# A gated MLP's first product with seven multiplications per block pair: running sums kept in PSUM, copied out between terms

## Chip, cores and metric

The kernel runs on one core of one Trainium2 chip. The metric is the device time of one execution in microseconds; lower is better. Three executions of the kernel before were timed.

## What is computed

The reference runs three layers one after the other on 8 sequences of 576 tokens: a memory attention over 8 heads of 64, a channel mix with token shift, and a gated MLP. The change touches the first product of the last one, `x @ w_in`, cut here to what matters:

```python
h = np.maximum(x @ w_in, 0.0)              # 576 x 512 times 512 x 1024, for each of 8 sequences
u, v = h[..., :512], h[..., 512:]
v_n = (v - mean(v)) / np.sqrt(var(v) + 1e-06)      # over the 512 columns
v_s = einsum('ts,bsd->btd', w_spatial, v_n) + b_spatial[None, :, None]
out = (u * v_s) @ w_out
```

## The kernel before

All matrix products are made in single precision from pairs of rounded values: each operand is split into a high and a low part, and a product is the sum of high times high, low times high and high times low (`three`, line 104). TensorE adds the terms up in a PSUM bank (`gemm`, line 95); `start=True` on the first matmul makes it overwrite the bank. A split (line 116) is a copy on ScalarE and a subtraction on VectorE.

The first 600 us hold the attention and the channel mix. The gated MLP follows, a sequence at a time: `uv(n)` makes the v half and then the u half of `x @ w_in`, `spatial` (line 975) the product over tokens, `project` (line 1003) the last product. Of each sequence 512 tokens go through `uv(b)`; the 64 left over from all eight are collected in one more call, `uv(B)`, called "rest", which runs behind sequence 0's. So there are nine calls, eighteen halves.

A half is two groups (`Group`, line 837), each a 256 x 512 by 512 x 512 product done with Winograd's form of Strassen's method: seven products of half-size blocks (128 x 256 by 256 x 256, numbered 1 to 7) in place of eight, and sums of them. A group's four results are c11 = 1 + 2, c12 = 1 + 6 + 5 + 3, c21 = 1 + 6 + 7 + 4 and c22 = 1 + 6 + 7 + 5, with numbers standing for products. `products` (line 940) runs over the seven in the order 1, 6, 2, 7, 5, 3, 4 and at each of these seven places over the two groups, so a half has fourteen steps. A step (line 844) is six matmuls of 128 x 128 by 128 x 256 into a bank of its own, taken from the eight in turn (`mm`), and then the sums in SBUF: product 1 is copied by ScalarE (line 854), product 5 too (line 862); products 6, 2, 7, 3 and 4 are added by VectorE (line 851) to what stands in SBUF; and product 5's copy is added to c12 and to c22 by GpSimd, or by VectorE in the u half of sequence 0 (`engine`, line 961).

When a v group is through, `done` (line 928) normalises its two row tiles (`layer_norm`, line 824: Relu, statistics, square root, and scaling on ScalarE and VectorE in turn, with one buffer for each small result) and splits them. These run while TensorE makes the u half. In the u half the result is only needed by the product over tokens.

After the third and the sixth place a chunk of the previous sequence's `project` (twelve matmuls of 288 columns) is put between as a filler. In the halves of sequence 0 and of "rest" there is none; there `turn` issues splits of the token weights and of the next operands. `load_x2` (line 601) fetches and splits the seven left or right operands; GpSimd makes the differences. `issue_after(copied[0].ins)` keeps some of the splits behind the last copy out of PSUM on ScalarE's queue. Apart from that the framework orders the instructions of each engine ahead of time, by their place in the program and by when it reckons them ready; each engine then runs its list strictly in that order, waiting on semaphores.

Of the kernel before, what the change touches and what calls it, by code (L numbers as in the profile page):

```python
# [12 lines left out]
ACTF = mybir.ActivationFunctionType  # L13
ALU = mybir.AluOpType
# [13 lines left out]
HALF = 256  # L28
# [15 lines left out]
def kernel(  # L44
# [18 lines left out]
    nc = tc.nc  # L63
# [9 lines left out]
    def bank(n):  # L73
        return ps.tile([128, 512], F32, tag=f"bank{n}", name=f"bank{n}")
# [17 lines left out]

        return tile_of(f"xs{n}", [128, 2 * HB if n == 7 else 4 * HALF], F32R)

    def gemm(out, pairs, part=0, parts=1):

        n = len(pairs)
        for i in range(part * n // parts, (part + 1) * n // parts):
            x = nc.tensor.matmul(  # L99
                out=out, lhsT=pairs[i][0], rhs=pairs[i][1], start=i == 0, stop=i == n - 1  # L100
            )
        return x

    def three(ah, al, bh, bl):

        return [*zip(ah, bh), *zip(al, bh), *zip(ah, bl)]
# [302 lines left out]
    mm = turns(0, 1, 2, 3)  # L409
# [62 lines left out]
    for c in ORDER:  # L472
        if c == "W":
            fetch_w_k()
        elif c == "w":
            part, ms = next(w_k_parts)
# [7 lines left out]
        elif c == "M":  # L484
# [3 lines left out]
                out=mu_sb[:, 2 * KC:], in0=mu_sb[:, 0:2 * KC], scalar1=-1.0, scalar2=1.0,  # L488
                op0=ALU.mult, op1=ALU.add,
            )  # L490
        else:
            n, late = "CKQDLR".index(c.upper()), c.islower()
# [32 lines left out]
    def w_in_steps():  # L525


        chunks = w_in.bitcast(U32).rearrange("(c p) f -> p c f", p=128)

        def parts_of(tag, parts):  # L530
            tiles = pair(tag, [128, 4096])
            wi_tiles.extend(tiles)
            parts.extend(t[:, 0:3584].rearrange("p (q c f) -> p q c f", q=7, c=2) for t in tiles)

        def add(out, a, b, op=ALU.subtract):
            nc.gpsimd.tensor_tensor(out=out, in0=a, in1=b, op=op)

        def part(p, half, j):
            f0 = p * DM + half * HALF + j * 128
            return chunks[:, :, 2 * f0:2 * f0 + 256]  # L540

        quads = tile_of("xT0", [128, 2, KC, HALF])
        for half in range(2):
            for j in range(2):
                load_f64(part(0, half, j), raw=quads[:, half, :, 128 * j:128 * j + 128])
                yield
                yield
        while not att_free:
            yield
        room = tile_of("asp", [128, 1792])  # L550
        parts_of("AT", wi_v)
        for j in range(2):
            at = []
            for half in range(2):
                at.append(load_f64(part(1, half, j)))
                yield
            (a11, a12), (a21, a22) = ((v[:, 0:2], v[:, 2:4]) for v in at)
            h, lo = (p[:, :, :, 128 * j:128 * j + 128] for p in wi_v)
            raw = room[:, 0:768].rearrange("p (q c f) -> p q c f", q=3, c=2)
            add(raw[:, 0], a21, a22, ALU.add)  # L560
            add(raw[:, 1], raw[:, 0], a11)
            add(raw[:, 2], a11, a21)
            for q, a in ((0, a11), (1, a12), (2, a22), (3, raw[:, 0]), (4, raw[:, 1]), (5, raw[:, 2])):
                split(a, h[:, q], lo[:, q])
                if q % 2:
                    yield
            add(raw[:, 0], a12, raw[:, 1])
            split(raw[:, 0], h[:, 6], lo[:, 6])
            yield
        a11, a12, a21, a22 = (quads[:, half, 2 * k:2 * k + 2] for half in range(2) for k in range(2))  # L570
        s1, s2, s4 = (room[:, 512 * n:512 * n + 512].rearrange("p (c f) -> p c f", c=2) for n in range(3))
        add(s1, a21, a22, ALU.add)
        add(a21, a11, a21)
        yield
        add(s2, s1, a11)
        add(s4, a12, s2)
        yield
        while not xT_free:
            yield
        chunks = w_out.bitcast(U32).rearrange("(c p) f -> p c f", p=128)  # L580
        wo_raw = tile_of("xT1", [128, KC, DM])
        for f0 in range(0, DM, 128):
            load_f64(chunks[:, :, 2 * f0:2 * f0 + 256], raw=wo_raw[:, :, f0:f0 + 128])
            yield
        while not w2_free:
            yield
        wo.extend(pair("W2", [128, KC, DM]))
        for c in range(KC):
            split(wo_raw[:, c], wo[0][:, c], wo[1][:, c])
            yield  # L590
        parts_of("W1", wi_u)
        for q, a in ((0, a11), (4, s2), (1, a12), (5, a21), (3, s1), (6, s4), (2, a22)):
            split(a, wi_u[0][:, q], wi_u[1][:, q])
            yield

# [5 lines left out]
    def load_x2(n):  # L601
# [33 lines left out]
        def put(q, x):  # L635
            ts[q] = place(q)

            with tc.issue_after(copied[0].ins) if rest or (n == 0 and xs_free) else nullcontext():
                split(x, *ts[q])

        if rest:
            for x in ((b11, 0, 0), (b21, 1, 0), (b12, 0, 1), (b22, 1, 1)):
                fetch_x2(*x)
            yield
            tiles = [tile_of(tag, [128, FC * HB], F32R) for tag in ("kh", "kl")]
            slots.update(zip((0, 1, 2, 4), [t[:, 4 * HALF * k:4 * HALF * (k + 1)] for t in tiles for k in range(2)]))
            put(0, b11)
            minus(b11, b12, b11)
            minus(b12, b22, b12)
            yield  # L650
            put(2, b22)
            minus(b22, b22, b11)
            yield
            put(4, b22)
            yield
            put(1, b21)
            minus(b21, b21, b22)
            yield
            while not late_free:
                yield  # L660
            yield
            put(5, b12)
            yield
            put(3, b11)
            yield
        else:
            for x in ((b12, 0, 1), (b11, 0, 0), (b21, 1, 0), (b22, 1, 1)):
                fetch_x2(*x)
            yield
            put(0, b11)  # L670
            minus(b11, b12, b11)
            yield
            put(1, b21)
            minus(b12, b22, b12)
            yield
            put(2, b22)
            minus(b22, b22, b11)
            yield
            put(4, b22)
            minus(b21, b21, b22)  # L680
            while not xs_free:
                yield
            while left_v:

                yield
            yield
            put(5, b12)
            yield
            put(3, b11)
            yield  # L690
        put(6, b21)
        x2s[n] = [ts[q] for q in range(7)]
# [94 lines left out]
    mm = turns(*range(8))  # L787
# [49 lines left out]
    class Group:  # L837

        def __init__(self, at, out, done, engine=nc.gpsimd):
            self.at, self.out, self.done, self.engine = at, out, done, engine

        def step(self, q):
            c11, c12, c21, c22 = self.out
            acc = bank(next(mm))[:, 0:HALF]
            a, b = self.at(q)
            gemm(acc, three(*a, *b))

            def add(engine, dst, x, y):  # L850
                engine.tensor_tensor(out=dst, in0=x, in1=y, op=ALU.add)  # L851

            if q == 1:
                copied[0] = nc.scalar.activation(out=c11, in_=acc, func=ACTF.Copy)
            elif q == 6:
                add(nc.vector, c12, acc, c11)
            elif q == 2:
                add(nc.vector, c11, acc, c11)
            elif q == 7:
                add(nc.vector, c21, acc, c12)  # L860
            elif q == 5:
                copied[0] = nc.scalar.activation(out=c22, in_=acc, func=ACTF.Copy)
                add(self.engine, c12, c22, c12)
                add(self.engine, c22, c22, c21)
            elif q == 3:
                add(nc.vector, c12, acc, c12)
            else:
                add(nc.vector, c21, acc, c21)
                self.done()


# [3 lines left out]
    def uv(n, fillers):  # L875
# [62 lines left out]
            return done  # L938

        def products(groups, after=lambda at_: None):  # L940
            for at_, q in enumerate((1, 6, 2, 7, 5, 3, 4)):
                for g in groups:
                    g.step(q)
                    turn()
                after(at_)
                if at_ in (2, 5):
                    f = next(fillers, None)
                    if f is not None:
                        f()
# [7 lines left out]
        def u_half(after=lambda at_: None):  # L957
            u = u_rest if rest else u_main
            products([
                Group(u_at(m), [u[:, f + m, s:s + HALF] for f in (0, 2) for s in (0, HALF)], lambda: None,  # L960
                      nc.vector if n == 0 else nc.gpsimd)
                for m in range(2)
            ], after)

# [183 lines left out]
```

## Time and profile before

| | |
|---|---|
| median of three runs | 1012.88 us (1010.77 to 1013.5) |
| span of the profiled execution | 1013.0 us |
| instructions | 20477 |
| TensorE matmuls, weight loads | 989.3 us (98%), 964.3 us (95%) |
| VectorE | 681.0 us (67%) |
| ScalarE | 608.5 us (60%) |
| GpSimd | 113.5 us (11%) |
| DMA | 87.83 MB, mean 87 GB/s |

The span runs from the first to the last instruction. PE stands for TensorE's matmuls, PEld for its weight loads, DVE for VectorE, ACT for ScalarE, POOL for GpSimd. Matmuls overlap: one of 256 columns has a row of 0.28 us, but the next starts some 0.11 us after it. A row of the timeline can merge several instructions of one form; "x4" says how many. What stands in brackets behind a row is the idle time before it and what ended it.

### The profile page before, as it was taken

Reading aid. Unit: us, or ns where it says so; the run is one execution under the profiler, and the core shown is the slowest. Engines: PE = TensorE matmul, PEld = TensorE weight load, DVE = VectorE, ACT = ScalarE, POOL = GpSimd, SP = SyncE. Lnnn points to the kernel's source line nnn. Section 1 sums busy time; section 2 is a strip of 40 time slices with the busy share of each in tenths; the row PEclk is TensorE's granted clock in tenths of the full one; section 3 lists DMA queues with packets and bytes.
Section 4 is the critical chain, followed back from the end, with each engine's and each line's share of the span. In section 5 each row is a group of like instructions: output and inputs, shape, how many; then the busy total and the mean of one; then the engine's idle time right before and its main releaser. Section 6 shows DMA issues by size and latency. Waiting matters only on the chain.

```text
span 1013.0 us, 20477 instructions
## 1 busy us (share of the span) xinstructions
PE 989.3 (98%) x8192; PEld 964.3 (95%) x8192; DVE 681.0 (67%) x1525; ACT 608.5 (60%) x1277; POOL 113.5 (11%) x124
## 2 busy tenths in 40 slices
PE   5889999999999999999999999999999999999998
PEld 4778999999999999999999999999999999999998
DVE  4999965675576567556667577986575757575763
ACT  4797885676678668657756475655354444445352
POOL 0000000000000000000022021412231313122220
PEclk9999999999999999999999999999999999999999
DMA  9686532233223322330042311202111111121101
GB/s 267 164 276 237 148 100 71 80 114 109 65 85 106 121 78 64 114 109 24 6 149 66 107 45 36 89 30 60 36 56 36 54 36 60 37 65 57 40 25 47
DMA packets 65135, 87.83 MB, mean 87 GB/s; under 512 B 8848, under 2 KB 57360, under 8 KB 62992
## 3 DMA queue, kind: packets, MB, share of 16 engines
q1 hardware_dynamic: 65040, 86.53, 27.6%
q8 instruction: 64, 1.05, 0.4%
q14 instruction: 31, 0.25, 0.1%
HBM read 67.77 MB, written 18.74 MB: 85 GB/s over the span
## 4 chain that ended last, share of the span: by engine, by line
PE 80%; ACT 8%; DVE 7%; DMA 3%; issue 1%; SPq 0%; POOL 0%; ACTq 0%; POOLq 0%; DVEq 0%
PE bank L99 77%; PE bank L271 2%; DMA st<-in_w_in 1%; DMA ATh<-in_kv 1%; DVE xs L118 1%; ACT t L712 1%; ACT kh L117 1%; ACT xs L117 1%; ACT t L710 1%; PE bank L323 1%; ACT xT L382 1%; DMA st<-x2d 0%; DVE kl L118 0%; ACT st L145 0%; ACT x32a L416 0%
## 5 line engine op out<-in xcount | busy, mean ns | idle before, releaser
L99 PE MATMUL bank<-xs,W1h 128*128 128x288 f32 (+1 forms) x1496 | 244.5, 292 | 1.8 <-DVE o L749 1.2
L99 PEld LDWEIGHTS bank<-xs,W1h 128*128 128x128 f32 x1496 | 210.4, 188 | 6.9 <-issue 5.8
L99 PE MATMUL bank<-xs,W1l 128*128 128x288 f32 (+1 forms) x748 | 135.5, 290 | 0.0
L99 PEld LDWEIGHTS bank<-xs,W1l 128*128 128x128 f32 x748 | 110.7, 188 | 0.2 <-issue 0.2
L118 DVE TENSOR_TENSOR kl<-t,kh 128x576 fp32r<-128x576 f32 x64 | 49.3, 771 | 58.5 <-ACT kh L117 57.9
L99 PE MATMUL bank<-xs,W2h 128*128 128x288 f32 x512 | 83.9, 298 | 1.3 <-ACT t L710 0.6
L710 ACT ACTIVATE t<-bank 128x288 f32<-128x288 f32 x128 | 50.8, 402 | 57.0 <-PE bank L99 56.6
L99 PE MATMUL bank<-kh,W3h 128*128 128x288 f32 x512 | 80.0, 297 | 1.5 <-ACT W3h L161 1.0
L99 PE MATMUL bank<-kh,W3l 128*128 128x288 f32 x512 | 80.6, 297 | 0.0
L99 PE MATMUL bank<-kl,W3h 128*128 128x288 f32 x512 | 79.2, 296 | 0.0
L99 PEld LDWEIGHTS bank<-xs,W2h 128*128 128x128 f32 x512 | 72.7, 189 | 4.6 <-issue 2.5
L99 PEld LDWEIGHTS bank<-kh,W3h 128*128 128x128 f32 x512 | 71.4, 189 | 4.1 <-ACT W3h L161 1.9
L99 PE MATMUL bank<-ATh,xs 128*128 128x256 f32 x472 | 73.6, 278 | 0.0
L99 PEld LDWEIGHTS bank<-kh,W3l 128*128 128x128 f32 x512 | 72.0, 189 | 0.8 <-issue 0.7
L99 PEld LDWEIGHTS bank<-kl,W3h 128*128 128x128 f32 x512 | 71.9, 189 | 0.0
L851 DVE TENSOR_TENSOR st<-bank,st 128x256 f32<-128x256 f32 x70 | 29.1, 424 | 63.4 <-PE bank L99 51.2
L118 DVE TENSOR_TENSOR xs<-st,xs 128x512 fp32r<-128x512 f32 (+1 forms) x60 | 54.9, 919 | 22.3 <-ACT xs L117 22.2
L117 ACT ACTIVATE xs<-st 128x512 fp32r<-128x512 f32 (+1 forms) x60 | 36.2, 624 | 49.9 <-POOL st L631 34.9
L99 PEld LDWEIGHTS bank<-ATh,xs 128*128 128x128 f32 x472 | 63.5, 188 | 0.0
L117 ACT ACTIVATE kh<-bank 128x288 fp32r<-128x288 f32 x64 | 26.0, 407 | 54.7 <-DVE bank L995 54.7
L1016 ACT ACTIVATE o<-bank 128x288 f32<-128x288 f32 x64 | 25.8, 403 | 42.7 <-PE bank L99 31.7
L371 POOL MEMSET xT<- 128x4 f32 x8 | 1.1, 133 | 434.2 <-DVE x32b L420 357.5
(270 smaller groups left out, 2212.6 us busy)
## 6 DMA issues: line engine op xcount, KB each, us to landing
ATh<-in_kv SPq DMA_DIRECT2D x14, 1300.0 KB, 6.1
out_T<-o SPq DMA_DIRECT2D x64, 144.0 KB, 1.7
ATl<-in_qT SPq DMA_DIRECT2D x30, 288.0 KB, 4.3
st<-x2d SPq DMA_DIRECT2D x32, 256.0 KB, 3.6
ATh<-in_phin SPq DMA_DIRECT2D x15, 320.0 KB, 3.2
x2d<-o SPq DMA_DIRECT2D x32, 144.0 KB, 2.0
st<-in_w_in SPq DMA_DIRECT2D x8, 512.0 KB, 4.2
ATh<-in_phiT SPq DMA_DIRECT2D x14, 288.0 KB, 2.9
```

The lines of the kernel that those rows point to most:

```text
L99: x = nc.tensor.matmul(out=out, lhsT=pairs[i][0], rhs=pairs[i][1], start=i == 0, stop=i == n - 1)
L117: high = nc.scalar.activation(out=h, in_=x, func=ACTF.Copy)
L118: nc.vector.tensor_tensor(out=lo, in0=x, in1=h.bitcast(F32), op=ALU.subtract)
L271: x = nc.tensor.matmul(out=kvp[32 * j:32 * j + 32, :], lhsT=ph[0:n, t, 32 * j:32 * j + 32], rhs=kv[0:n, t, j, :], start=(t == 0), stop=(t ...
L323: x = nc.tensor.matmul(out=scs[hf][32 * j:32 * j + 32, :], lhsT=kmT[64 * hf:64 * hf + 64, 32 * j:32 * j + 32], rhs=q[64 * hf:64 * hf + 64, ...
L371: nc.gpsimd.memset(xT[b][:, :, 0:1], 0.0)
L382: nc.scalar.activation(out=xT[b][:, 2 * g + pr, 1 + hf * HB:1 + (hf + 1) * HB], in_=xo, func=ACTF.Copy)
L710: nc.scalar.activation(out=ks[:, m % 2 * HB:(m % 2 + 1) * HB], in_=acc, func=ACTF.Relu)
L712: nc.scalar.activation(out=ks, in_=ks, func=ACTF.Square)
L851: engine.tensor_tensor(out=dst, in0=x, in1=y, op=ALU.add)
L1016: nc.scalar.activation(out=o, in_=acc, func=ACTF.Copy)
```

## The change

One bank now holds a running sum. Product 1 goes into bank x and is copied to c11; product 6 is added onto it by TensorE and the sum copied to c12; product 7 is added and the sum copied to c22; product 4 is added and the sum copied to c21. Product 2 has bank z and is added to c11. Product 5 goes into bank y, which VectorE adds to c22, and product 3 is then added onto it, and VectorE adds the sum to c12. The copies are ScalarE's, the three adds VectorE's; GpSimd has none. A half takes six banks in place of fourteen turns. The order of the products becomes 1, 2, 6, 5, 7, 4, 3; a group is done after 3 and not after 4; and the operands are split in the new order.

```diff
-    def gemm(out, pairs, part=0, parts=1):
+    def gemm(out, pairs, part=0, parts=1, fresh=True):
...
-                out=out, lhsT=pairs[i][0], rhs=pairs[i][1], start=i == 0, stop=i == n - 1
+                out=out, lhsT=pairs[i][0], rhs=pairs[i][1], start=fresh and i == 0, stop=i == n - 1,
+                skip_group_check=not fresh,
...
-        for q, a in ((0, a11), (4, s2), (1, a12), (5, a21), (3, s1), (6, s4), (2, a22)):
+        for q, a in ((0, a11), (1, a12), (4, s2), (3, s1), (5, a21), (2, a22), (6, s4)):
             split(a, wi_u[0][:, q], wi_u[1][:, q])
...
+            put(3, b11)
+            yield
             put(5, b12)
-            yield
-            put(3, b11)
             yield
...
         def step(self, q):
             c11, c12, c21, c22 = self.out
-            acc = bank(next(mm))[:, 0:HALF]
+            if q == 1:
+                self.x = bank(next(mm))[:, 0:HALF]
+            elif q == 2:
+                self.z = bank(next(mm))[:, 0:HALF]
+            elif q == 5:
+                self.y = bank(next(mm))[:, 0:HALF]
+            acc = self.z if q == 2 else self.y if q in (5, 3) else self.x
             a, b = self.at(q)
-            gemm(acc, three(*a, *b))
-
-            def add(engine, dst, x, y):
-                engine.tensor_tensor(out=dst, in0=x, in1=y, op=ALU.add)
+            gemm(acc, three(*a, *b), fresh=q in (1, 2, 5))
+
+            def keep(dst):
+                copied[0] = nc.scalar.activation(out=dst, in_=acc, func=ACTF.Copy)
+
+            def add(dst, x):
+                nc.vector.tensor_tensor(out=dst, in0=x, in1=dst, op=ALU.add)
 
             if q == 1:
-                copied[0] = nc.scalar.activation(out=c11, in_=acc, func=ACTF.Copy)
+                keep(c11)
+            elif q == 2:
+                add(c11, acc)
             elif q == 6:
-                add(nc.vector, c12, acc, c11)
-            elif q == 2:
-                add(nc.vector, c11, acc, c11)
+                keep(c12)
             elif q == 7:
-                add(nc.vector, c21, acc, c12)
-            elif q == 5:
-                copied[0] = nc.scalar.activation(out=c22, in_=acc, func=ACTF.Copy)
-                add(self.engine, c12, c22, c12)
-                add(self.engine, c22, c22, c21)
+                keep(c22)
+                add(c22, self.y)
+            elif q == 4:
+                keep(c21)
             elif q == 3:
-                add(nc.vector, c12, acc, c12)
-            else:
-                add(nc.vector, c21, acc, c21)
+                add(c12, acc)
                 self.done()
...
-            for at_, q in enumerate((1, 6, 2, 7, 5, 3, 4)):
+            for at_, q in enumerate((1, 2, 6, 5, 7, 4, 3)):
```

The two `put` lines change places in both branches of `load_x2`, and the `engine` argument of `Group` goes away.

## Rows read from the trace of the kernel before

**Rows 1.** The page, parts 1 and its head: span, TensorE's busy time.

```profile
span 1013.0 us, 20477 instructions
...
PE 989.3 (98%) x8192; PEld 964.3 (95%) x8192; DVE 681.0 (67%) x1525; ACT 608.5 (60%) x1277; POOL 113.5 (11%) x124
```

**Rows 2.** Waits of TensorE's matmuls, 540 to 1013 us: total, times, longest.

```profile
PE bank L99 <- ACT kh L117: 1.1, 1, 1.1
```

**Rows 3.** Busy time by stretch: length, PE, PEld, DVE, ACT, POOL, clock, DMA share, GB/s.

```profile
640.00:670.00 30.00, 28.88 (x229) 28.64 (x228) 28.50 (x64) 15.44 (x31) 12.36 (x12) 1.00 0.11 36
```

**Rows 4.** Timeline of a v half (sequence 2): TensorE, ScalarE, weight loads; start, length.

```profile
728.48 0.62 PE L99 MATMUL bank<-ATh,xs 128*128 128x256 f32 x4
729.16 0.62 PE L99 MATMUL bank<-ATh,xs 128*128 128x256 f32 x4
...
728.68 0.38 ACT L862 ACTIVATE st<-bank 128x256 f32<-128x256 f32 x1 [1.59 <-PE bank L99]
...
729.05 0.30 PEld L99 LDWEIGHTS bank<-ATh,xs 128*128 128x128 f32 x2
```

**Rows 5.** Timeline of the u half behind it: third matmuls of the seventh and eleventh steps.

```profile
739.54 0.40 PE L99 MATMUL bank<-xs,W1l 128*128 128x256 f32 x2
...
742.37 0.40 PE L99 MATMUL bank<-xs,W1l 128*128 128x256 f32 x2
```

**Rows 6.** Chain of work that ended last, 640 to 670 us, in order of time.

```profile
648.27 4.97 DMA st<-x2d
...
667.04 0.31 ACT kh L117
667.35 0.04 issue
667.39 2.66 PE bank L99 x18
```

**Rows 7.** Groups by line and form, 600 to 1013 us: count, busy us, mean ns, idle before.

```profile
L862 ACT ACTIVATE xT<-bank 128x256 f32<-128x256 f32 x20 | 7.3, 371 | 5.2 <-PE bank L99 5.2
...
L851 DVE TENSOR_TENSOR xT<-bank,xT 128x256 f32<-128x256 f32 x100 | 39.9, 412 | 9.2 <-POOL xT L851 6.5 <-PE bank L99 2.5
...
L851 POOL TENSOR_TENSOR xT<-xT 128x256 f32<-128x256 f32 x36 | 29.2, 821 | 100.4 <-ACT xT L862 99.0
```

**Rows 8.** Timeline of ScalarE around the fifth place of that u half.

```profile
741.69 0.82 ACT L835 ACTIVATE st<-st,nb,sd 128x512 f32<-128x512 f32 x1 [0.79 <-DVE nb L834]
742.41 0.36 ACT L862 ACTIVATE xT<-bank 128x256 f32<-128x256 f32 x1
742.67 0.62 ACT L117 ACTIVATE W3h<-st 128x512 fp32r<-128x512 f32 x1
...
743.38 0.37 ACT L862 ACTIVATE xT<-bank 128x256 f32<-128x256 f32 x1
744.69 0.82 ACT L835 ACTIVATE st<-st,nb,sd 128x512 f32<-128x512 f32 x1 [0.94 <-DVE nb L834]
```

**Rows 9.** Timelines of ScalarE and TensorE in three early halves (rest v, rest u, sequence 1's v).

```profile
638.87 0.64 ACT L862 ACTIVATE xs<-bank 128x256 f32<-128x256 f32 x2
649.12 0.66 ACT L862 ACTIVATE xT<-bank 128x256 f32<-128x256 f32 x2
...
679.12 0.66 ACT L854 ACTIVATE st<-bank 128x256 f32<-128x256 f32 x2 [0.52 <-DVE xs L118]
...
638.24 0.64 PE L99 MATMUL bank<-ATh,kl 128*128 128x256 f32 x4
...
648.12 0.39 PE L99 MATMUL bank<-kl,W1h 128*128 128x256 f32 x2
...
676.30 0.63 PE L99 MATMUL bank<-ATh,xs 128*128 128x256 f32 x4
```

**Rows 10.** Timeline of TensorE at the change to the gated MLP.

```profile
600.86 0.63 PE L99 MATMUL bank<-ATh,xs 128*128 128x256 f32 x4
601.63 0.53 PE L99 MATMUL bank<-kh,W3h 128*128 128x288 f32 x2
```

More of the change, by code (lines that the diff above doesn't have):

```diff
@@ L686, in load_x2 @@
             yield
+            put(3, b11)
+            yield
             put(5, b12)
-            yield
-            put(3, b11)
             yield
@@ L837, with __init__ @@
     class Group:
-        def __init__(self, at, out, done, engine=nc.gpsimd):
-            self.at, self.out, self.done, self.engine = at, out, done, engine
+        def __init__(self, at, out, done):
+            self.at, self.out, self.done = at, out, done
         def step(self, q):
             c11, c12, c21, c22 = self.out
-            acc = bank(next(mm))[:, 0:HALF]
-            a, b = self.at(q)
-            gemm(acc, three(*a, *b))
-            def add(engine, dst, x, y):
-                engine.tensor_tensor(out=dst, in0=x, in1=y, op=ALU.add)
+            if q == 1:
[5 more added lines that the diff above has]
+            acc = self.z if q == 2 else self.y if q in (5, 3) else self.x
+            a, b = self.at(q)
+            gemm(acc, three(*a, *b), fresh=q in (1, 2, 5))
[3 more added lines that the diff above has]
+                nc.vector.tensor_tensor(out=dst, in0=x, in1=dst, op=ALU.add)
             if q == 1:
-                copied[0] = nc.scalar.activation(out=c11, in_=acc, func=ACTF.Copy)
+                keep(c11)
+            elif q == 2:
+                add(c11, acc)
             elif q == 6:
-                add(nc.vector, c12, acc, c11)
-            elif q == 2:
-                add(nc.vector, c11, acc, c11)
+                keep(c12)
             elif q == 7:
-                add(nc.vector, c21, acc, c12)
-            elif q == 5:
-                copied[0] = nc.scalar.activation(out=c22, in_=acc, func=ACTF.Copy)
-                add(self.engine, c12, c22, c12)
-                add(self.engine, c22, c22, c21)
+                keep(c22)
+                add(c22, self.y)
+            elif q == 4:
+                keep(c21)
             elif q == 3:
-                add(nc.vector, c12, acc, c12)
-            else:
-                add(nc.vector, c21, acc, c21)
+                add(c12, acc)
                 self.done()
@@ L959, in u_half @@
             products([
-                Group(u_at(m), [u[:, f + m, s:s + HALF] for f in (0, 2) for s in (0, HALF)], lambda: None,
-                      nc.vector if n == 0 else nc.gpsimd)
+                Group(u_at(m), [u[:, f + m, s:s + HALF] for f in (0, 2) for s in (0, HALF)], lambda: None)
                 for m in range(2)
```

## The prediction, made before the changed kernel was run

> **What bounds the kernel now.** I read the page's busy times first, then TensorE's waits in the second half of the span, then the stretch around the one wait found there, and last the timelines of two halves of the gated MLP, engine by engine.
>
> TensorE is busy for 989.3 of 1013.0 us [rows 1]. All that the change touches lies behind 600 us, and from 540 us to the end TensorE waits once, for 1.1 us, on ScalarE's `kh` at line 117 [rows 2]. That wait falls into the stretch from 640 to 670 us, where VectorE is busy 28.5 of 30 us and TensorE 28.9 [rows 3]. Everywhere else matmuls follow each other without a gap, so the gated MLP is bound by TensorE: work taken off the other engines earns only what it takes out of that 1.1 us, and every wait put in front of a matmul is paid in full.
>
> The margin in which the change lives can be read off one half. A half has fourteen steps: seven places in the order, each with a step for group 0 and one for group 1. A step is six matmuls and takes 0.68 us (728.48 to 729.16 [rows 4]) or 0.71 (four steps from 739.54 to 742.37 [rows 5]). A product's last matmul starts 0.11 us before the next step and takes 0.28, the copy on ScalarE starts 0.04 after its end and takes 0.38 (728.68 in [rows 4]); ScalarE's end reaches TensorE after 0.05 (667.35 in [rows 6]).
>
> **The change, part by part.**
>
> *Fewer adds on VectorE and GpSimd, more copies on ScalarE.* Per group the operations fall from nine to seven: copies from two to four, adds out of PSUM from five to three, adds in SBUF from two to none. There are 36 groups. VectorE loses 76 adds of 0.41 us [rows 7], 31 us; GpSimd loses 68 (72 less the four that block 0's u half had on VectorE) of about 0.82, some 55 us; ScalarE gains 72 copies of 0.37, 27 us on top of its load. None of this is on the path: TensorE covers all of it, since it waits for none of these engines outside that one place. I cost it at nothing. If the cover fails it does so for ScalarE, the engine that gets more; that is the part after next.
>
> *The 1.1 us.* The chain into this wait runs from the landing of `x2d` at 653.24 (issued once VectorE's splits had freed its tile) through splits and norms on VectorE and ScalarE to `kh` at 667.04 [rows 6]. In the halves from 621 to 651 us VectorE loses at least twelve adds, 5 us, so the tile comes free sooner. Bounds: -1.1 (gone) and 0 (the transfer still lands last). I take -1.1, because 5 us less in front of a 1.1 us wait is ample.
>
> *Reuse of a bank in the middle of a half.* Before, each step takes the next of eight banks, so a slow copy has eight steps to get out of the way. Afterwards product 6 is added onto product 1's bank, product 7 onto that and product 4 onto that, so each must wait until ScalarE has copied what stands there. In the order 1, 2, 6, 5, 7, 4, 3 these pairs stand at places 1 and 3, 3 and 5, 5 and 6. The first two leave at least three steps, 2 us, against 0.47 for a copy and its signals. The last leaves one step. That is the place to price, and the kernel before has a copy at the very same place: product 5 stands fifth there and line 862 copies it, as product 7 will be copied now.
>
> In a v half, group 0's copy is through at 728.68 + 0.38 + 0.05 = 729.11 us; the weight load of the sixth place begins at 729.05 [rows 4]. It would be 0.06 late. Group 1 is then shifted by as much and adds nothing. Seven such halves (all but the two treated below): 0.4 us. The bounds are 0 and 0.06 each; I take the upper, because nothing competes for ScalarE there.
>
> The Trainium skill, "PSUM — Partial Sum Buffer", section "PSUM bank collisions raise a hardware error", says that TensorE writing a bank while another engine reads it is an error that the hardware does not hold back, and that semaphores must guard whole banks. By that rule the term waits for the end of the copy, as priced here; could it follow behind the copy's first columns, the v halves would cost nothing and the sum would be 0.4 lower. No row of the kernel before can show it, as no bank there is written again after it was read in mid-half.
>
> In a u half ScalarE is still normalising the v half. At the fifth place of the half at 733 us the copy of group 0 starts behind a 0.82 us operation and that of group 1 behind a split [rows 8]. The sixth place begins at 742.37 - 0.24 = 742.13 [rows 5], its weight load 0.11 earlier. The copies end, with 0.05, at 742.82 and 743.80: late by 0.80 and, against 742.73, by 1.07. So the bounds for a u half are 0.03 (the copy is prompt) and 1.07 (order and times on ScalarE stay). Both can move, since the copies are new instructions in a new order and the first norm of each half can begin sooner: its `c21` is copied after the sixth place instead of being added after the seventh. I take a copy that arrives at a random moment of the 3.0 us between two norms (741.69 to 744.69): it meets the 0.82 and the 0.62 us operation and waits (0.82² + 0.62²) / (2 x 3.0) = 0.18 us on average. With 0.06 of its own and half of 0.18 for the second copy that makes 0.33. Seven u halves: 2.3 us; bounds 0.2 and 7.5.
>
> Three halves at the start have late copies for reasons of their own. Read in the same way [rows 9]: 638.87 + 0.42 against 638.13, 1.2 us; 649.12 + 0.42 against 648.01, 1.5; and, at the first place, whose bank is needed at the third, 679.12 + 0.43 against 676.19, 3.4. Bounds: 0 and 6.1. I take 1.0, near the lower end. When a product's operands are late, the issuing order gives TensorE matmuls of others: at 600.86 four matmuls of a v product stand among those of `kh` and W3 [rows 10]. In the half at 676 us two steps of product 5 and a chunk of the projection are ready to be put there, about 3 us of work.
>
> *VectorE's `c22` plus product 5* must come before product 3 is added onto that bank. It is ready 0.4 us after the copy of product 7, takes 0.41, and has two steps (and mostly a projection chunk of 1.6 us) to do it: nothing in the regular halves; in the two early ones it is inside the 1.0.
>
> *Reordered splits* of W1 and of x2 follow the new order one for one; each is issued no later against its first use than before. Nothing. *Adding onto a bank* instead of starting afresh: five of six matmuls of a step add already and all six are equally spaced, so nothing.
>
> **Sum.** -1.1 + 0.4 + 2.3 + 1.0 = +2.6 us on a span of 1013.0, 1015.6. The span of the profiled execution is 0.1 above the median of 1012.88, so the forecast in time is 1015.5. A measurement of this kernel tells apart about 0.3%, 3 us; the forecast lies inside that.
>
> **Rivals.**
>
> *The waits at the sixth place open in full (slower).* Place: u halves, product 4 behind the copy of product 7. Price: 7 x 1.07 = 7.5, with 0.4 and 1.0 as above and the 1.1 not regained: +8.9, 1021.8 us. For it: the rows show just this lateness, and in the same size in each of the seven halves, because ScalarE's order is fixed ahead of time. Against: that lateness was free before, so nothing pressed the order. It decides once ScalarE's copies in u start more than about 0.4 us after the product. If the early halves stay in full too the end is 1013.0 + 14.0 = 1027. Chance of slower by over 0.3%: 0.38.
>
> *TensorE's pace changes (faster).* Steps with equal columns take 0.68 us in one half and 0.71 in another [rows 4, 5], at a granted clock of 1.00 [rows 3], and nothing in the rows says why. If the nine u halves (126 steps) went at the quicker pace, that is 126 x 0.0275 = 3.5 us; with the 1.1 gone and waits of 0.8 in all: -3.8, 1009 us. Against: the slow pace sets in with the first u step in almost every half, and the operands of u do not change. Chance of faster by over 0.3%: 0.20.
>
> *The relief is hidden and the waits are filled too (no change).* The issuing order moves other ready matmuls into each gap, and only the 0.4 and -1.1 are left: 1012.2. This and the forecast share the middle: 0.42, of which the forecast has the larger part.
>
> **How the numbers follow.** Forecast 1015.5. The range goes from just below the faster rival, 1008.5, to just above the slower one, 1022.5; outside lie the full bound of 14 us and a change of pace on top of everything else, together less than 2 in 10.
>
> **What would show it.** GpSimd has no adds at all from the gated products, and VectorE's busy time falls by about 31 us: right whatever the time does. TensorE's waits should name ScalarE's copies of products 7, up to nine times at 0.06 to 1.1 us; if each of them is near 1 us the first rival is right, if there are none the third. The `kh` wait near 667 us should be gone. The step time in u of 0.71 shows whether the pace moved. The prediction is wrong if waits on VectorE's add into `c22` appear in regular halves, or if the norms come so late that the spatial products wait for them.

## The result: 0.7% slower, and the profile after

The changed kernel takes 1021.03 us (median of 5 runs, 1018.47 to 1022.43) against 1013.5 of the kernel before, run beside it: a ratio of 1.0073, 95% interval 1.0054 to 1.0092, or 7.4 us (5.5 to 9.3). The time lies inside the range of the prediction, but it is the time of the first rival (1021.8) and not of the forecast (1015.5).

The page's head and busy times [rows 1]:

```profile
span 1019.2 us, 20282 instructions
...
PE 992.5 (97%) x8192; PEld 966.0 (95%) x8192; DVE 660.8 (65%) x1449; ACT 634.1 (62%) x1349; POOL 62.1 (6%) x56
```

The work moved as the diff says: VectorE has 76 instructions fewer, GpSimd 68 fewer, ScalarE 72 more. The groups by line and form from 600 us on (count, busy us, mean ns, idle before) answer to [rows 7]:

```profile
L858 ACT ACTIVATE xT<-bank 128x256 f32<-128x256 f32 x80 | 29.1, 374 | 9.1 <-PE bank L99 9.1
L861 DVE TENSOR_TENSOR xT<-bank,xT 128x256 f32<-128x256 f32 x60 | 24.6, 417 | 12.6 <-ACT xT L858 9.3 <-PE bank L99 2.9
```

One operation costs what it did (copies 0.37, adds 0.42). No GpSimd group of adds is left. The busiest engine that is not TensorE has been relieved, and TensorE waits more. Its waits from 540 us to the end [rows 2], total, times, longest:

```profile
PE bank L99 <- ACT xT L858: 4.8, 8, 0.9
PE bank L99 <- ACT xs L858: 0.5, 1, 0.5
PE bank L99 <- ACT kh L118: 0.2, 1, 0.2
```

The 1.1 us on `kh` in sequence 0 are gone; the 0.2 that is listed is at 600.26 us, where the kernel before has the same gap (0.14 us, ahead of the second row of [rows 10]). In their place stand nine waits on line 858, the copies of the running sum. Seven stand one in each u half of sequences 1 to 7, with 0.53 to 0.57 us of idle TensorE, and look like the one in the u half of [rows 5, 8]; two stand in "rest". Here is ScalarE there, in the changed kernel (line 832 is the norm's square root, 836 its scaling):

```profile
742.01 0.28 ACT L832 ACTIVATE sd<-mv,eps 128x1 f32<-128x1 f32 x1
742.24 0.39 ACT L858 ACTIVATE xT<-bank 128x256 f32<-128x256 f32 x1
743.19 0.81 ACT L836 ACTIVATE st<-st,nb,sd 128x512 f32<-128x512 f32 x1 [0.56 <-DVE nb L835]
743.91 0.36 ACT L858 ACTIVATE xT<-bank 128x256 f32<-128x256 f32 x1
```

and TensorE in the same stretch:

```profile
742.51 0.67 PE L99 MATMUL bank<-xs,W1h 128*128 128x256 f32 x4
...
743.24 0.39 PE L99 MATMUL bank<-xs,W1h 128*128 128x256 f32 x2
743.46 0.29 PE L99 MATMUL bank<-kh,W2h 128*128 128x288 f32 x1
744.32 0.50 PE L99 MATMUL bank<-xs,W1h 128*128 128x256 f32 x2 [0.56 <-ACT xT L858]
```

Group 0's copy of product 7 starts at 742.24 and is in time to 0.04 us. Group 1's product 7 ends with the first two of the four matmuls at 742.51, so its copy could start near 742.95. It starts at 743.91, because in ScalarE's list the scaling stands ahead of it, and ScalarE has stood still for 0.56 us until VectorE's `nb` was there. TensorE is through with product 4 of group 0 after the two matmuls at 743.24; product 4 of group 1 is next. It has one matmul of the projection to put in (743.46), and then nothing until 744.32. The chain of work that ended last says the same from the other side, 742 to 746 us:

```profile
742.14 0.69 DVE W3l L119
742.83 0.08 DVE sd L833
...
742.94 0.22 DVE nb L835
...
743.19 0.81 ACT st L836
744.00 0.28 ACT xT L858
744.28 0.04 issue
744.32 1.76 PE bank L99 x12
```

For a while the matmuls of u hang on the norm of v, which no matmul of u needs.

How much that is per sequence is read from the start of one sequence's product over tokens to the next one's, a period without noise from the first 600 us. Timeline of TensorE, its first matmuls in sequences 1 and 2, in the kernel before:

```profile
699.45 0.55 PE L99 MATMUL bank<-asp,W3h 128*128 128x288 f32 x3
...
746.56 0.56 PE L99 MATMUL bank<-asp,W3h 128*128 128x288 f32 x3
```

and in the changed one:

```profile
699.93 0.56 PE L99 MATMUL bank<-asp,W3h 128*128 128x288 f32 x3
...
748.00 0.56 PE L99 MATMUL bank<-asp,W3h 128*128 128x288 f32 x3
```

47.11 against 48.07 us: 0.96 more. The other five later periods of each kernel are the same to 0.03. The first period (from sequence 0 to 1) was 48.52 and is 48.05; it held the `kh` wait, worth 1.41 (48.52 less 47.11). From the first matmul of the gated MLP to sequence 0's product over tokens it is 50.8 before (600.15 to 650.93) and 53.1 after (598.76 to 651.88): 2.3 more. What follows the last period is 30.9 in both. The sum: 7 x 0.96 - 1.4 + 2.3 = +7.6 us, against 7.4 measured.

Of the 2.3, 0.8 and 1.2 lie in the v and the u half of "rest" (9.87 and 9.90 us before, 10.67 and 11.14 after) [rows 9], and 0.3 in sequence 0. Timeline of ScalarE and TensorE in "rest" (line 929 is a split of the 64 rows left over):

```profile
637.05 0.45 ACT L118 ACTIVATE ATh<-st 128x288 fp32r<-128x288 f32 x1
637.39 0.39 ACT L858 ACTIVATE xs<-bank 128x256 f32<-128x256 f32 x1
...
637.82 0.74 PE L99 MATMUL bank<-ATh,xs 128*128 128x256 f32 x4 [0.47 <-ACT xs L858]
...
647.21 1.28 ACT L929 ACTIVATE W3l<-xs 64x512 fp32r<-64x512 f32 x2
648.52 0.38 ACT L858 ACTIVATE xT<-bank 128x256 f32<-128x256 f32 x1
...
648.95 0.51 PE L99 MATMUL bank<-xs,W1h 128*128 128x256 f32 x2 [0.94 <-ACT xT L858]
```

The second copy stands behind a split, the first behind a row of splits of the token weights, of which the one at 637.05 is the last.

### The profile page after: what moved, and what is told of

The parts are those of the page before. It is cut to its first block, busy times and chain, and to the rows that moved or that the text cites. A ratio compares the mean times of both kernels' runs of the same rounds, so it can differ in the third digit from the quotient of the medians.

```text
span 1019.2 us, 20282 instructions
## 1 busy us (share of the span) xinstructions
PE 992.5 (97%) x8192; PEld 966.0 (95%) x8192; DVE 660.8 (65%) x1449; ACT 634.1 (62%) x1349; POOL 62.1 (6%) x56
## 4 chain that ended last, share of the span: by engine, by line
PE 71%; ACT 12%; DVE 10%; DMA 3%; issue 2%; SPq 0%; POOL 0%; ACTq 0%; POOLq 0%; DVEq 0%
PE bank L99 68%; PE bank L272 2%; ACT st L836 2%; DVE W3l L119 1%; DVE st L828 1%; ACT W3h L118 1%; DMA st<-in_w_in 1%; DMA ATh<-in_kv 1%; DVE xs L119 1%; ACT t L713 1%; ACT xs L118 1%; ACT t L711 1%; PE bank L324 1%; ACT kh L118 1%; DVE nb L835 1%
## 5 line engine op out<-in xcount | busy, mean ns | idle before, releaser
L119 DVE TENSOR_TENSOR xs<-st,xs 128x512 fp32r<-128x512 f32 (+1 forms) x60 | 57.4, 968 | 24.3 <-ACT xs L118 23.7
L118 ACT ACTIVATE xs<-st 128x512 fp32r<-128x512 f32 (+1 forms) x60 | 36.8, 627 | 44.9 <-POOL st L632 29.3
L861 DVE TENSOR_TENSOR st<-bank,st 128x256 f32<-128x256 f32 x42 | 17.8, 425 | 69.6 <-ACT st L858 36.7
L99 PE MATMUL bank<-ATl,xs 128*128 128x256 f32 x236 | 46.6, 279 | 0.0
```

The costliest lines, as they stand in the source:

```text
L99: x = nc.tensor.matmul(out=out, lhsT=pairs[i][0], rhs=pairs[i][1], start=fresh and i == 0, stop=i == n - 1, skip_group_check=not fresh,)
L118: high = nc.scalar.activation(out=h, in_=x, func=ACTF.Copy)
L119: nc.vector.tensor_tensor(out=lo, in0=x, in1=h.bitcast(F32), op=ALU.subtract)
L861: nc.vector.tensor_tensor(out=dst, in0=x, in1=dst, op=ALU.add)
```

## The experiments

The theory: TensorE's loss is the copy of product 7 being late in ScalarE's strict order, behind norm operations, with one step between it and the next use of its bank. The rivals: copy and signals are by themselves too long for one step; VectorE's add is what is late; the loss has nothing to do with the bank. The table gives every run: the time from the first gated matmul to sequence 1's product over tokens, the usual later period, both from start times of matmuls as above, and the ratio to the kernel before.

| kernel | to sequence 1, us | later period, us | ratio (95%) |
|---|---|---|---|
| before | 99.30 | 47.11 | |
| changed | 101.17 | 48.07 | 1.0073 (1.0054 to 1.0092) |
| 1 filler between 7 and 4 | 100.57 | 47.11 | 1.0005 (0.9989 to 1.0021) |
| 2 product 4 in its own bank | 102.83 | 47.38 | 1.0059 (1.0037 to 1.0082) |
| 3 scaling on VectorE | 101.52 | 48.02 | 1.0075 (1.0054 to 1.0096) |
| 4 before, GpSimd's adds on VectorE | 98.52 | 47.11 | 0.9985 (0.9969 to 1.0001) |
| 5 no norm | 100.87 | 47.25 | 1.0014 (0.9999 to 1.0030) |
| 6 copy of 7 on VectorE | 100.62 | 47.90 | 1.0074 (1.0058 to 1.0090) |
| 7 two tight pairs | 102.48 | 48.31 | 1.0101 (1.0080 to 1.0123) |
| 8 filler, bank per product early | 100.41 | 47.11 | 1.0037 (1.0020 to 1.0053) |
| 9 the same, sequence 1 too | 98.69 | 47.11 | 0.9991 (0.9974 to 1.0008) |
| 10 bank per product early only | 98.20 | 48.07 | 1.0059 (1.0038 to 1.0080) |

**1. The filler between the tight pair.** The twelve matmuls of a projection chunk move from behind product 4 to in front of it:

```diff
-                if at_ in (2, 5):
+                if at_ in (2, 4):
```

> The changed kernel with the second filler (a chunk of the previous sequence's projection, 1.6 us) put before product 4 instead of behind it. Theory W (the added time is TensorE waiting at product 4 for ScalarE's copy of product 7): the copy gets 1.6 us more, the seven waits of about 0.9 us in the u halves and the 0.1 us in the v halves go, and only the two early halves without fillers keep theirs, about 2 us: 1013.5 to 1015.5 us. Rival S (the time comes with the adding onto a bank, with the order of products or with ScalarE's greater load, wherever the filler stands): 1019 to 1022 us.

1014.19 us against 1013.63, a ratio of 1.0005. The period is the one of the kernel before to 0.01 us in six of seven sequences (the one of sequence 5 to 6 is 47.45; run 9 comes back to it). All that TensorE still waits for, 540 us to the end:

```profile
PE bank L99 <- ACT xs L858: 1.0, 1, 1.0
PE bank L99 <- ACT xT L858: 0.9, 1, 0.9
```

Both are in "rest", which has no filler. In the regular halves the copies are still not prompt. ScalarE, timeline:

```profile
741.44 0.64 ACT L858 ACTIVATE xT<-bank 128x256 f32<-128x256 f32 x2
742.62 0.82 ACT L836 ACTIVATE st<-st,nb,sd 128x512 f32<-128x512 f32 x1 [0.55 <-DVE nb L835]
```

By the ends of their products the two copies could start near 740.7 and 741.4; they start at 741.44 and, behind each other, some 0.3 us later. ScalarE's list has changed as well: both now stand ahead of this scaling, where the second stood behind it. But product 4 of the second group is due 2 us behind the end of its product 7, and even the copy that was 0.96 us late in the changed kernel would be through by then. There is 1.6 us of other work in front of whoever needs the copies.

**2. Product 4 in its own bank.** It takes a fresh bank; VectorE adds it to `c22` as it stands (1 + 6 + 7) for `c21`, and then adds product 5:

```diff
-            gemm(acc, three(*a, *b), fresh=q in (1, 2, 5))
+            gemm(acc, three(*a, *b), fresh=q in (1, 2, 5, 4))
...
-                keep(c21)
+                nc.vector.tensor_tensor(out=c21, in0=acc, in1=c22, op=ALU.add)
+                add(c22, self.y)
```

> The changed kernel with one part undone: product 4 gets a bank of its own and VectorE adds it to c22 in SBUF (before product 5 is added there) to make c21; products 6, 7 and 3 still go onto running sums. Theory W: nothing waits for product 7's copy any more one step later, so about 1013 to 1015 us, also in the early halves. Rival S (any running sum costs): most of the 7.5 us stays, 1018 to 1021 us.

1018.98 us: above what was expected. The period is back within 0.27 of the old one, so the tight pair is most of it there. But the early part got worse. TensorE's waits, 540 us to the end:

```profile
PE bank L99 <- DVE xs L861: 1.0, 1, 1.0
PE bank L99 <- DVE xT L861: 0.9, 1, 0.9
PE bank L99 <- ACT st L858: 0.6, 1, 0.6
...
```

VectorE now stands between product 5 and product 3, as ScalarE did between 7 and 4, and in "rest" it is just as late. The third wait is a copy of product 1 in sequence 1's v half, at the place that the prediction bounded at 3.4 us [rows 9].

**3. The scaling on VectorE.** The long norm operation that stands ahead of the copy leaves ScalarE:

```diff
-        nc.scalar.activation(out=v, in_=v, func=ACTF.Identity, bias=nb, scale=sd)
+        nc.vector.tensor_scalar(out=v, in0=v, scalar1=sd, scalar2=nb, op0=ALU.mult, op1=ALU.add)
```

> The changed kernel with the last operation of each row's normalisation (times sd plus nb, 0.82 us on ScalarE) moved to VectorE; the running sums are untouched. Theory W in the form that this scaling stands in front of the copy on ScalarE's queue: in the u halves the copy comes at most 0.6 us late (a split can still stand there), waits fall from 0.9 to between 0 and 0.4 us, 1014 to 1017.5 us. Rival (the wait has its length from the copy and its signals alone, or from VectorE): no change, 1020 to 1022 us.

1020.4 us, no gain; the rival's time. ScalarE's timeline shows why:

```profile
746.45 0.63 ACT L118 ACTIVATE W3h<-st 128x512 fp32r<-128x512 f32 x1 [0.54 <-DVE st L836]
746.99 0.64 ACT L858 ACTIVATE xT<-bank 128x256 f32<-128x256 f32 x2
```

The split of the scaled rows (line 118) has come to the scaling's place: again an operation that waits for VectorE (0.54 us), and the copy behind it. It is not the scaling that is too long, it is the norm's chain, which crosses between the two engines and stands still in ScalarE's queue.

**4. The relief without the running sums.** In the kernel before, GpSimd's adds go to VectorE:

```diff
-                Group(v_at(k), [v[a + k][:, b:b + HALF] for b in (0, HALF) for a in (0, 2)], v_done(k))
+                Group(v_at(k), [v[a + k][:, b:b + HALF] for b in (0, HALF) for a in (0, 2)], v_done(k), nc.vector)
...
-                      nc.vector if n == 0 else nc.gpsimd)
+                      nc.vector)
```

> The kernel before with GpSimd's adds of product 5 moved to VectorE in every half; banks, order and copies as before. It measures what the relief of GpSimd and VectorE is worth: VectorE gets some 68 adds of 0.41 us more than before, 28 us. My account (these adds lie beside TensorE's work): 1013 to 1015 us, no difference. Rival (GpSimd's adds cost something through shared access, or VectorE's load is near the bound): below 1011 or above 1016 us.

1012.25 us, 0.9985 (0.9969 to 1.0001). The period is unchanged, and the 1.1 us on `kh` are gone in its profile although VectorE has more to do (a wait of 0.3 us on a copy in sequence 1 stands there, and the first period is 47.72). So in this execution at least it was not VectorE's load that decided over `kh`. Taking GpSimd out is worth that wait at most, with the running sums or without them.

**5. No norm.** In the seven regular sequences `layer_norm` is left out:

```diff
-                        layer_norm(v[t])
```

> The changed kernel without the normalisation of v in the seven regular sequences (its split stays, so ScalarE still copies and splits while TensorE makes the u half; the computation leaves the normalisation out there). Theory: product 4 waits because the copy of product 7 stands, in ScalarE's fixed order, behind a norm operation that itself waits for VectorE. Without the norms the copies of product 7 start within 0.1 us of their product, TensorE waits at the sixth place for at most 0.1 us, the period from spatial product to spatial product goes from 48.07 to about 47.2 us, and the time is 1014.5 to 1016 us, since the waits of the early halves (some 2 us) stay. Rival: the copy with its signals is by itself too long for one step, or ScalarE's splits alone delay it: the period stays near 48 us and the time at 1020 us.

1014.46 us and a period of 47.25, both as the theory has them. ScalarE at the same place, timeline:

```profile
741.25 0.38 ACT L858 ACTIVATE xT<-bank 128x256 f32<-128x256 f32 x1 [0.32 <-PE bank L99]
```

The copy at 741.25 waits for the product and for nothing else. Of the 0.96 us per sequence the norm is 0.82 (48.07 less 47.25); copy and signals alone are the other 0.14.

**6. The copy of product 7 on VectorE.**

```diff
-                keep(c22)
+                nc.vector.tensor_copy(out=c22, in_=acc)
```

> The changed kernel with the copy of product 7's running sum made by VectorE in place of ScalarE. Theory: it leaves ScalarE's queue, where it stood behind the norm's scaling, but VectorE's queue is as strictly in order and has the norm's small steps that wait for ScalarE's square root; the copy is late by 0 to 0.7 us in place of 0.86, the period is 47.1 to 47.9 us and the time 1014 to 1019 us. Rival: TensorE's wait at the sixth place comes from the single step between the two products and not from ScalarE's queue; then nothing changes and the time stays at 1020 to 1022 us.

1020.78 us. The period of 47.90 is the upper end of what was expected, the time is the rival's; the rows decide between them. The wait has changed its name and its group. VectorE, then TensorE:

```profile
742.27 0.69 DVE L119 TENSOR_TENSOR W3l<-st,W3h 128x512 fp32r<-128x512 f32 x1 [1.48 <-ACT W3h L118]
742.88 0.16 DVE L833 RECIPROCAL sd<-sd 128x1 f32<-128x1 f32 x1
742.95 0.41 DVE L870 COPY xT<-bank 128x256 f32<-128x256 f32 x1
...
743.41 0.50 PE L99 MATMUL bank<-xs,W1h 128*128 128x256 f32 x2 [0.37 <-DVE xT L870]
```

Now group 0's copy is late, behind a split that waits 1.48 us for ScalarE. Either of the two engines that share the norm has a queue that stands still at this time.

**7. Two tight pairs.** Product 6 moves next to product 7, so that 6, 7 and 4 follow each other on one bank:

```diff
-            for at_, q in enumerate((1, 2, 6, 5, 7, 4, 3)):
+            for at_, q in enumerate((1, 2, 5, 6, 7, 4, 3)):
```

> The changed kernel in the order 1, 2, 5, 6, 7, 4, 3: now product 7 also comes one step after product 6, so two pairs on the running sum are one step apart in place of one. Theory: each tight pair whose copy stands behind a norm operation on ScalarE costs up to 0.9 us per sequence; with two of them the period goes from 48.07 to between 48.3 and 49.3 us and the time to 1022.5 to 1030 us, with waits on the copies of product 6 as well. Rival: the loss has nothing to do with how many steps lie between a copy and the next use of its bank; the time stays at 1020 to 1022 us.

1022.89 us, a period of 48.31: slower by as much as the lower end of what was expected. TensorE in the u half:

```profile
742.14 0.50 PE L99 MATMUL bank<-xs,W1h 128*128 128x256 f32 x2 [0.47 <-ACT xT L858]
...
743.86 0.50 PE L99 MATMUL bank<-xs,W1h 128*128 128x256 f32 x2
...
744.42 0.74 PE L99 MATMUL bank<-xs,W1h 128*128 128x256 f32 x4
```

The large wait is now between 6 and 7 (742.14). The pair 7 and 4 costs little more: the first wait has put TensorE back so far that the next copies find the norms nearly over. Here the late copies did not add up; the first one paid for most of those behind it.

**8 to 10. What is left.** Run 8 has the filler of run 1, and in sequence 0 and "rest", which have none, a bank per product and sums in SBUF, all on VectorE:

```diff
+            if not self.kept:
+                acc = bank(next(mm))[:, 0:HALF]
...
-                if at_ in (2, 5):
+                if at_ in (2, 4):
...
-                Group(u_at(m), [u[:, f + m, s:s + HALF] for f in (0, 2) for s in (0, HALF)], lambda: None)
+                Group(u_at(m), [u[:, f + m, s:s + HALF] for f in (0, 2) for s in (0, HALF)], lambda: None, 0 < n < B)
```

> The changed kernel with the second filler put between products 7 and 4 (as in the first of the earlier runs), and with sequence 0 and the rest, which have no filler, back to a bank per product and sums in SBUF (all adds on VectorE) in the new order. Theory: the regular sequences keep a period of 47.11 us, the early halves lose their waits of about 1 us each, the first part goes from 53.4 to about 50.8 us, and the time is 1012 to 1013.5 us: equal to the kernel before or up to 0.15% below it. Rival: VectorE, which now carries the adds of the early halves beside the splits, becomes late there and the time stays at 1014 to 1016 us.

1015.44 us, above what was expected, although the waits of "rest" are gone and the period is 47.11. One wait has opened in their stead, in sequence 1's v half. ScalarE and TensorE there, timelines:

```profile
679.28 0.63 ACT L118 ACTIVATE xs<-st 128x512 fp32r<-128x512 f32 x1 [0.38 <-DVE W3l L957]
680.72 0.66 ACT L885 ACTIVATE st<-bank 128x256 f32<-128x256 f32 x2 [0.82 <-DVE xs L119]
...
681.16 0.73 PE L99 MATMUL bank<-ATh,xs 128*128 128x256 f32 x4 [1.88 <-ACT st L885]
```

These are the copies of product 1 behind the splits of "rest", whose bank product 6 wants two places later: the third early half of the prediction. The changed kernel has no wait at this place; runs 2, 3 and 4 have 0.6, 0.4 and 0.3 us. What decides it is not shown: waits further ahead are not it alone, since run 2 has more of them than the changed kernel. By the trace, from the first gated matmul on, the kernel is 1.4 us behind the one before, by the runs 3.7 (2.0 to 5.4). The executions differ in their granted clock, and part of the gap is there (last section): between those at 1.00 it is 2.6 us in the medians. Another 0.3 lies outside the span; the rest is not explained. Run 9 gives sequence 1 a bank per product as well (`1 < n < B`); run 10 does that with the filler left where the change has it.

> As the run before it (filler between products 7 and 4, a bank per product in sequence 0 and the rest), with sequence 1 back to a bank per product as well, so that six of the nine calls keep the running sums. Theory: the wait of 1.9 us of sequence 1's v half is a copy of product 1 that stands behind the rest's norm on ScalarE and whose bank product 6 wants two places later; with a bank per product there nobody waits for it, every period from spatial product to spatial product is 47.1 to 47.3 us, no wait of TensorE over 0.3 us is left behind 600 us, and the time is 1012 to 1014 us, level with the kernel before. Rival: the wait is for something else that comes late at that place (the rest's norm, which everything behind it would feel); then the first period stays near 49.3 us and the time at 1015 to 1016 us.

1012.67 us, 0.9991 (0.9974 to 1.0008): level with the kernel before, and no wait on a copied bank is left:

```profile
PE bank L99 <- ACT kh L118: 1.2, 2, 1.1
PE bank L99 <- DVE xs L119: 0.2, 1, 0.2
```

The expectation of no wait over 0.3 us was missed: 1.1 on `kh`, as in [rows 2], but in a later sequence (903 us). As in [rows 6], the chain into it starts with a transfer of `x2d`, and ScalarE waits long for that:

```profile
889.48 0.63 ACT L118 ACTIVATE xs<-st 128x512 fp32r<-128x512 f32 x1 [3.52 <-DMA st<-x2d]
```

In four other sequences the same wait is 1.2 to 1.8 us, and in run 1 it is 2.5 in the one whose period is 47.45. Why the transfer landed later there stays open.

> The changed kernel with the filler left where it was, between products 4 and 3, and sequence 0, the rest and sequence 1 back to a bank per product. If the terms add, the early waits go (first part near 50.8 us, no wait of about 1 us there) and the first period, of sequence 1, falls to 47.1 to 47.3 us, while the six later periods stay at 48.07 us: 6 x 0.96 = 5.8 us above a kernel without waits, 1017.5 to 1019.5 us. Rival: the waits of the regular halves depend on what the early halves left on ScalarE's queue; then the later periods move away from 48.07 us.

1020.26 us, a little above what was expected; the ratio of 1.0059 is 6.0 us (3.9 to 8.1). The two executions at a granted clock of 1.00, of which the profiled one is one, took 1015.7 and 1016.4 us, the five below it 1020.0 to 1021.5, so the median says less than the trace, which is 4.9 us behind the kernel before from the first gated matmul on. The trace has what the theory asked for: no early wait, a first period of 47.13, and six later ones at 48.06 to 48.07, the changed kernel's to 0.01. Here the terms of the early and the regular halves did not depend on each other.

## Why the prediction was partly right

**The step that failed** is the price of the u halves: "I take a copy that arrives at a random moment of the 3.0 us between two norms", 0.33 us each. Two things are wrong in it. ScalarE's list is fixed, so the copy meets the same neighbour in every sequence; there was no average to take, only one value between the bounds of 0.03 and 1.07, the same in all seven halves. Measured as the prediction does, end of the copy against the due weight load, it is 0.97 in sequence 2 (744.32 against 743.35), less 0.13 for the filler matmul put in between; run 5 puts 0.82 per sequence on the norm. And the average counted only the time in which ScalarE is busy. The queue also stands still while the scaling waits for `nb`, and [rows 8] show 0.94 us of that in front of 0.82 us of work. With these 1.76 us in one piece the same formula gives (1.76² + 0.62²) / (2 x 3.0) = 0.58. (The 0.06 that it adds for a prompt copy is the v half's; by its own reading the u half's is 0.03. That is 0.2 us in all.)

**By terms**, predicted and measured: the `kh` wait -1.1, -1.4 (48.52 less 47.11). V halves +0.4 and u halves +2.3; measured 7 x 0.96 = +6.7, of which 7 x 0.14 = +1.0 is what run 5 leaves for copies and signals in both halves, and 7 x 0.82 = +5.7 goes with the norm. Early halves +1.0, measured +2.3. Together +2.6 and +7.6. That the -1.1 came out is in part luck: its reason was VectorE's relief, and in run 4 the wait goes with more load on VectorE.

**The v halves** wait as read from [rows 4]. Timeline after, sequence 2 (copy, then weight load, then matmuls):

```profile
729.17 0.38 ACT L858 ACTIVATE st<-bank 128x256 f32<-128x256 f32 x1 [1.59 <-PE bank L99]
...
729.61 0.53 PEld L99 LDWEIGHTS bank<-ATh,xs 128*128 128x128 f32 x4
...
729.65 0.69 PE L99 MATMUL bank<-ATh,xs 128*128 128x256 f32 x4
```

729.17 + 0.38 + 0.05 is 729.60, and the load starts at 729.61. TensorE waits for the end of the copy, and some 0.1 us are lost over the two groups (from 728.98 to the filler at 731.13 it is 2.15 us, before from 728.48 to 730.52 2.04), where 0.06 were predicted. The same is seen at 744.28 to 744.32 in the chain. The Trainium skill, "PSUM — Partial Sum Buffer", section "PSUM bank collisions raise a hardware error", has semaphores guard a whole bank, and the trace agrees: in both places TensorE's first row into the bank comes 0.04 us or more behind the end of the copy. No run here shows a collision.

**The early halves:** two of the three opened, with 0.47 and 0.94 us of idle matmuls; the issuing order put nothing into them. The third did not open; in runs 2, 3 and 8 it did, with 0.6, 0.4 and 1.9 us. The bound of 6.1 was thus real, the choice of 1.0 too low by the assumed filling.

**The rivals.** The first one named the place, the reason and roughly the size of the waits in u: "the rows show just this lateness, and in the same size in each of the seven halves, because ScalarE's order is fixed ahead of time". What was held against it, that nothing had pressed the order, did not count: under pressure the order only gave one filler matmul (743.46). That its 1021.8 us lies next to the measured 1021.03 is partly luck: it kept the `kh` wait (+1.4 against the measured sum) and had the u halves higher (7.5 against 5.7), the early ones lower (1.0 against 2.3) and the v halves with the prompt copies at 0.4 against 1.0. The second, pace, did not happen: third matmuls of u steps stand at 734.33, 735.04, 735.75, 0.71 apart as in [rows 5]. But the pace can change within a half: steps of sequence 0's v half start 0.68 us apart from 606.05 to 610.81 and 0.70 to 0.71 from 611.57 on, where before they are 0.68 to the end of the half. What sets it stays open. The third, filled gaps, failed by that one matmul; run 1 shows that it would have been right for the regular halves had the chunk stood one place earlier.

**The relief** came nearly as counted. The adds out of PSUM fell from 180 rows with 72.9 us (three groups by tile, [rows 7] and two smaller) to 108 rows with 44.9, 28.0 us, and four in SBUF are gone; but VectorE's busy time fell by 20.2 and not by 31. Some 2.5 us of it are the 60 splits of the operands, longer in this execution (54.9 to 57.4 us); the rest was not taken apart. ScalarE gained 25.6 of 27, and GpSimd lost 51.4 of 55. All this was off the path, as argued, and the 1.4 us regained is the most that it paid (run 4 regains that wait without the running sums). VectorE's add into `c22` was not waited for in any regular half, and the product over tokens did not wait for the norms.

## What to carry to other kernels

When a result is to stay in PSUM and be copied out between two terms, the copy joins the path: look at what stands ahead of it in the copying engine's queue, count the time in which that queue stands still as well as its busy time, and do it for each place once, since the list does not change from one round to the next. If the accumulating step must follow closely, put other matmuls between by hand, as run 1 did; taking the work to another engine helps only if that engine's queue moves at that time. A less loaded VectorE or GpSimd was worth here at most the one wait that the kernel before shows.

## What was not expected of the hardware

A wait costs more than its idle time. After one, the first two matmuls take 0.50 us (744.32) where two otherwise take 0.39 or 0.40 (743.24): the weight load starts together with the matmul, not ahead of it, and 0.11 us are lost again. TensorE's weight loads, timeline:

```profile
744.32 0.30 PEld L99 LDWEIGHTS bank<-xs,W1h 128*128 128x128 f32 x2 [0.78 <-ACT xT L858]
```

The prediction had this in its prices, since it measured lateness against the weight load and not against the matmul; a list of TensorE's waits leaves it out. The Trainium skill, "PSUM — Partial Sum Buffer", section "Engine vs sequencer instructions", has ScalarE's and VectorE's queues strictly first in, first out, while TensorE can load weights during running matmuls; the trace agrees on the first with every late copy above, and on the second as long as matmuls run (loads at [rows 4] lie 0.1 us ahead of their matmuls): after a wait there is none to load under.

The profiled executions took 1.8 us longer than their spans (1021.03 and 1019.2 us after, 1014.23 and 1012.4 in run 1, 1012.3 and 1010.5 in run 4); in runs 6 and 8 to 10 it is 2.0 to 2.1. The one of the kernel before, with a span of 1013.0, is therefore better put near 1014.8 than at the median, as the prediction had it; its sum, being a difference, does not change.

The first matmul of the gated MLP starts anywhere from 596.0 (run 10) to 602.9 us (run 8), behind code that these kernels share but for the order of W1's splits. One span against another thus hides 7 us, and only the periods told 0.1 us apart.

The granted clock is part of that noise. Of the executions of the kernel before that were timed beside runs 1 to 4, the ten with a mean granted clock of 1.00 took 1011.2 to 1013.6 us, the seven with 0.995 took 1015.5 to 1016.8. In the profiles the clock is below 1.00 only in the first 100 us, long before the change: in the kernel before it is 0.50 (1.2 of 2.4 GHz) from 14 to 16 us, after 3 us without a matmul; in runs 1 and 10 it never falls there. Executions at 1.00 compared with each other come nearer to the traces: run 1 is then 1.6 us behind the kernel before in the medians (1013.5 and 1011.9), as it is in its trace from the first gated matmul to the end (414.45 us against 412.85), and not the 0.5 of its ratio.
